# Instruction order from a list scheduler written into the kernel, and two chunks first through the up projection

## The chip, the cores and the metric

The kernel runs on one core of one Trainium2 chip. The metric is the device time of one execution in microseconds (us), median of several. One run at a time is profiled; its span (first to last instruction) is some 2 us shorter than its time. TensorE is PE in the profile, VectorE DVE, ScalarE ACT, GpSimd POOL, the engine that issues most transfers SP.

## The reference, cut to what matters

```python
# attention (RWKV-6): batch 4, 8 heads, 768 steps, head size 48, all fp32
for t in range(S):
    cur = u * k_t (outer) v_t
    y[:, :, t] = r_t @ (state + cur)
    state = w_t * state + k_t (outer) v_t
# then an MLP on x = y laid out as (3072, 384)
h = x @ w_in                       # 384 x 2048, weights given as float64
g = h * clip(h + 3, 0, 6) / 6      # hardswish
out = g @ w_out                    # 2048 x 384
```

## The kernel before

Time is cut into 24 chunks of 128 steps (six to a batch element); three chunks make a block, 8 blocks in all. Per chunk there are two scans and some multiplications (the *preparation*), small matmuls for scores, state and output (the *attention*), and then, block by block, the MLP: 16 *ups* with a gate each, and 16 *downs* per chunk. The MLP's weights come as 64-bit words and are turned into fp32 in the kernel, 16 pairs of 128-row or 128-column blocks, three VectorE steps and two ScalarE steps a pair:

```python
nc.scalar.activation(out=more, in_=lo, func=ACT.Copy, bias=2.0 ** 23, scale=2.0 ** -29)
nc.scalar.activation(out=more.bitcast(I32), in_=more, func=ACT.Copy, bias=-2.0 ** 23, scale=1.0)
nc.vector.tensor_scalar(out=top, in0=hi, ...)                    # shift
nc.vector.scalar_tensor_tensor(out=top, in0=hi, in1=top, ...)    # join
nc.vector.tensor_tensor(out=dst, in0=top, in1=more.bitcast(I32), op=ALU.add)   # full
```

The output of the attention has four head pairs. Three leave PSUM straight into the MLP's input `xT`; the fourth goes to a tile `x3` first, and small DMAs, here called *moves*, bring its rows to the partitions where they belong:

```python
for g in range(2):
    nc.scalar.copy(out=xT[rows, :, now], in_=y_ps[rows, 0:NCC, :])
    nc.scalar.copy(out=x3[rows, now], in_=y_ps[rows, P - 1, :])
if c == BC - 1 or i == 0:                      # chunk 0 alone, else once a block
    for g in range(2):
        for j in range(NCC):
            q = nc.scalar if i == 0 and g == 1 else nc.sync
            q.dma_start(out=xT[to:to + X3, j, cols], in_=x3[...])
```

The order at the start is written by hand, and the framework's own scheduler reorders it:

```python
prep(0); attend(0); prep(1); convert_next(); attend(1)
up(0, 0, 0, 1); up(0, 1, 0, 1)                 # block 0's ups: chunk 0 alone first
prep(2); convert_next(); up(0, 2, 0, 1); up(0, 3, 0, 1); convert_next(); attend(2)
# ... then the rest of block 0 between conversions, and for every chunk i from 3 on:
#     attend(i) with pieces of MLP between its parts, then prep(i + 1)
```

Of the kernel before, what the change touches and what calls it, by code (L numbers as in the profile page):

```python
# [8 lines left out]
F32 = mybir.dt.float32  # L9
# [12 lines left out]
BC = 3  # L22
LEAST = 2.0 ** -60
# [42 lines left out]
def fast_weights(nc, io, wk, w_in, w_out, moe_w_in, moe_w_out):  # L66



    bits_of = {}  # L70

    def fetch(which, f):
        if which == "in":
            srcs = [moe_w_in[:, (f + x) * 128:(f + x + 1) * 128].rearrange("(c p) j -> p c j", p=128) for x in range(2)]
            dst = w_in[:, f:f + 2].rearrange("p f c j -> p (f c) j")
        else:
            srcs = [moe_w_out[(f + x) * 128:(f + x + 1) * 128, :].rearrange("p (c j) -> p c j", j=128)
                    for x in range(2)]
            dst = w_out[:, f:f + 2].rearrange("p f (c j) -> p (f c) j", j=128)
        m = dst.shape[1] // 2  # L80
        if srcs[0].dtype == F32:
            for x in range(2):
                nc.sync.dma_start(out=dst[:, x * m:(x + 1) * m], in_=srcs[x])
            return
        bits = io.tile([128, 2 * m * 128], I64, name="bits", bufs=3)
        for x in range(2):
            nc.sync.dma_start(out=bits.rearrange("p (c j) -> p c j", j=128)[:, x * m:(x + 1) * m], in_=srcs[x])
        bits_of[which, f] = bits, dst.rearrange("p c j -> p (c j)").bitcast(I32)

    def convert(which, f):  # L90
        if (which, f) not in bits_of:
            return
        bits, dst = bits_of.pop((which, f))
        n = dst.shape[1]
        lo = bits.bitcast(U32).rearrange("p (j two) -> p j two", two=2)[:, :, 0]
        hi = bits.bitcast(I32).rearrange("p (j two) -> p j two", two=2)[:, :, 1]
        top = wk.tile([128, n], I32, name="top")
        more = wk.tile([128, n], F32, name="more")

        nc.scalar.activation(out=more, in_=lo, func=ACT.Copy, bias=2.0 ** 23, scale=2.0 ** -29)  # L100
        nc.scalar.activation(out=more.bitcast(I32), in_=more, func=ACT.Copy, bias=-2.0 ** 23, scale=1.0)
        nc.vector.tensor_scalar(out=top, in0=hi, scalar1=3, scalar2=0x3FFFFFF8,  # L102
                                op0=ALU.logical_shift_left, op1=ALU.bitwise_and)
        nc.vector.scalar_tensor_tensor(out=top, in0=hi, scalar=-0x40000000, in1=top,  # L104
                                       op0=ALU.bitwise_and, op1=ALU.bitwise_or)
        nc.vector.tensor_tensor(out=dst, in0=top, in1=more.bitcast(I32), op=ALU.add)  # L106

    return fetch, convert


def fast_path(tc, feat, tok, wflat, ub, moe_w_in, moe_w_out, out, flag, n_chunks):

# [11 lines left out]
    MB = BC * L  # L124
    X3 = D // NCC

    with ExitStack() as ctx:
# [4 lines left out]
        pp = ctx.enter_context(tc.tile_pool(name="pp", bufs=2, space=PSUM))  # L132

        st = [dict() for _ in range(NT)]

        def load(i):
            a = io.tile([PR, nf], F32, name="feat_in")
            b = io.tile([L, 3, HD], F32, name="tok_in", bufs=4)
            n = P * L
            if i == 0:  # L140
                nc.sync.dma_start(out=a[:, 2 * n:], in_=feat[i, :, 2 * n:])
                nc.scalar.dma_start(out=a[:, :2 * n], in_=feat[i, :, :2 * n])
            else:
                nc.sync.dma_start(out=a, in_=feat[i])
            nc.sync.dma_start(out=b.rearrange("s c e -> s (c e)"), in_=tok[i].rearrange("s c e -> s (c e)"))
            st[i].update(r=a[:, :n].rearrange("q (p t) -> q p t", p=P),
                         k=a[:, n:2 * n].rearrange("q (p t) -> q p t", p=P), w=a[:, 2 * n:],
                         rt=b[:, 0], kt=b[:, 1], v=b[:, 2].rearrange("s (h d) -> s h d", d=D))

        load(0)  # L150
        u_bc = const.tile([128, HD], F32, name="u_bc")
        nc.sync.dma_start(out=u_bc, in_=ub.to_broadcast([128, HD]))
        load(1)

        w_in = const.tile([128, NFC, NCC, 128], F32, name="w_in")
        w_out = const.tile([128, NFC, DM], F32, name="w_out")
        fetch, convert = fast_weights(nc, io, wk, w_in, w_out, moe_w_in, moe_w_out)

        fetches = [(which, f) for which in ("in", "out") for f in range(0, NFC, 2)]
        conversions = list(fetches)  # L160

        def fetch_next():
            if fetches:
                fetch(*fetches.pop(0))

        def convert_next():
            convert(*conversions.pop(0))
            fetch_next()

        fetch_next()  # L170
        load(2)
        fetch_next()
        fetch_next()

        ident = const.tile([128, 128], F32, name="ident")
        make_identity(nc, ident)
        half = const.tile([128, 1], F32, name="half")
        nc.vector.memset(half, 0.5)
        ones = const.tile([128, 1], F32, name="ones")
        nc.vector.memset(ones, 1.0)  # L180


        mask_f = const.tile([128, L], F32, name="mask_f")
        nc.gpsimd.memset(mask_f, 1.0)
        nc.gpsimd.affine_select(out=mask_f, in_=mask_f, compare_op=ALU.is_gt, fill=0.0, base=0,
                                pattern=[[1, L]], channel_multiplier=-1)
        mask = const.tile([128, L], U8, name="mask")
        nc.vector.tensor_copy(out=mask, in_=mask_f)


        back = const.tile([PR, P, L + 1], F32, name="back")
        nc.vector.memset(back, 0.0)
        nc.vector.memset(back[:, :, L:], 1.0)
        starts = []
        for i in range(2):
            b = const.tile([PR, P, L + 1], F32, name=f"start_{i}")
            nc.vector.memset(b, 0.0)
            starts.append(b)


        states = []
        for i in range(2):
            b = const.tile([PR, P, PR], F32, name=f"state_{i}")
            nc.gpsimd.memset(b, 0.0)
            states.append(b)


        VN = 1536
        n_w = wflat.shape[1] // VN
        n_v = DM * DFF // 128 // (VN // 2)  # L210
        w_max = const.tile([128, n_w], F32, name="w_max")
        w_min = const.tile([PR, NT, P], F32, name="w_min")
        f64 = moe_w_in.dtype != F32
        word_max = const.tile([128, 2, n_v], F32, name="word_max")
        word_min = const.tile([128, 2, n_v], F32, name="word_min")

        def vet_w(j):
            t = io.tile([128, VN], F32, name="bits", bufs=3)
            nc.sync.dma_start(out=t, in_=wflat[:, j * VN:(j + 1) * VN])
            nc.vector.tensor_reduce(out=w_max[:, j:j + 1], in_=t, axis=AX.X, op=ALU.max, apply_absolute_value=True)  # L220

        def vet_weights(which, j):
            n = VN // 2
            t = io.tile([128, n], I64, name="bits", bufs=3)
            src = (moe_w_in, moe_w_out)[which].rearrange("(p a) b -> p (a b)", p=128)
            nc.sync.dma_start(out=t, in_=src[:, j * n:(j + 1) * n])
            hi = t.bitcast(F32).rearrange("p (j two) -> p j two", two=2)[:, :, 1]
            for o, op in ((word_max, ALU.max), (word_min, ALU.min)):
                nc.vector.tensor_reduce(out=o[:, which, j:j + 1], in_=hi, axis=AX.X, op=op, apply_absolute_value=True)

        vets = [(vet_w, j) for j in range(n_w)]
        if f64:
            vets += [(vet_weights, which, j) for which in range(2) for j in range(n_v)]

        def prep(i):
            d = st[i]
            eng = nc.vector if i < BC else nc.gpsimd
# [3 lines left out]
                                         initial=0.0, op0=ALU.mult, op1=ALU.add)  # L241
            E = E_.rearrange("q (p t) -> q p t", p=P)
            start = starts[i % 2]
            nc.vector.reciprocal(out=start[:, :, 0:1], in_=E[:, :, 0:1])
            W_ = wk.tile([PR, P * (L + 1)], F32, name="W", bufs=3)
            nc.vector.tensor_tensor_scan(out=W_, data0=d["w"][:, :-1], data1=start.rearrange("q p t -> q (p t)"),  # L246
                                         initial=0.0, op0=ALU.mult, op1=ALU.add)
# [560 lines left out]
```

## Time and profile before

| what | value |
|---|---|
| time, median (range) | 649.93 us (648.22 to 650.29) |
| span of the profiled run | 646.3 us |
| last gap of TensorE at the start ends | 109.42 us |
| VectorE busy until then | 98.81 us |
| TensorE from there to its end | 531.43 us, busy 531.41 |
| copy and store after it | 5.45 us |

The slices, windows, waits and groups that carry this are shown in the prediction. Here are the moves, by their tile. The first number of a row is the shortest, then the median and the longest issue in ns; the last line is the time from issue to landing.

```profile
L348 SPq DMA_DIRECT2D xT<-x x15: 512/587/638, 23.8 to 98.3; - x15
L348 ACTq DMA_DIRECT2D xT<-x x3: 600/601/857, 24.5 to 26.0; - x3
DMA to landing us min/median/max: 1.7/1.9/3.6
```

At the median they land in 1.9 us.

### The profile page before, as it was taken

Reading aid. Unit: us, or ns where it says so; the run is one execution under the profiler, and the core shown is the slowest. Engines: PE = TensorE matmul, PEld = TensorE weight load, DVE = VectorE, ACT = ScalarE, POOL = GpSimd, SP = SyncE. Lnnn points to the kernel's source line nnn. Section 1 sums busy time; section 2 is a strip of 40 time slices with the busy share of each in tenths; the row PEclk is TensorE's granted clock in tenths of the full one; section 3 lists DMA queues with packets and bytes.
Section 4 is the critical chain, followed back from the end, with each engine's and each line's share of the span. In section 5 each row is a group of like instructions: output and inputs, shape, how many; then the busy total and the mean of one; then the engine's idle time right before and its main releaser. Section 6 shows DMA issues by size and latency. Waiting matters only on the chain.

```text
span 646.3 us, 7370 instructions
## 1 busy us (share of the span) xinstructions
PE 608.9 (94%) x2802; PEld 392.8 (61%) x2802; DVE 284.0 (44%) x414; ACT 216.8 (34%) x533; POOL 126.3 (20%) x118
## 2 busy tenths in 40 slices
PE   2667997999999999999999999999999999999996
PEld 2556875566656666666666666666666666555553
DVE  7988999769853343314412434115520133002200
ACT  1775874044221443133320443132430332102200
POOL 4135423432222122112121231131210000000000
PEclk9898999999999999999999999999999999999999
DMA  9678767999860221131130221210100000000000
GB/s 261 192 228 258 221 221 246 325 273 315 285 241 34 71 81 54 48 104 34 48 101 14 91 80 35 66 62 0 38 9 25 13 1 1 21 26 0 1 14 28
DMA packets 23900, 67.27 MB, mean 104 GB/s; under 512 B 2912, under 2 KB 13120, under 8 KB 23856
## 3 DMA queue, kind: packets, MB, share of 16 engines
q1 hardware_dynamic: 23632, 66.23, 32.2%
q8 instruction: 24, 0.39, 0.2%
q10 hardware_dynamic: 224, 0.48, 0.2%
q14 instruction: 20, 0.16, 0.1%
HBM read 60.81 MB, written 4.72 MB: 101 GB/s over the span
## 4 chain that ended last, share of the span: by engine, by line
PE 86%; DVE 6%; DMA 2%; ACT 2%; issue 1%; POOL 1%; ACTq 0%; SPq 0%; DVEq 0%
PE mm L374 38%; PE mm L355 35%; PE ps L334 3%; PE a_ps L270 3%; PE ps L329 2%; PE ps L295 2%; DMA feat_in<-in_feat_dram 1%; PE ps L284 1%; DVE top L102 1%; DVE w_out L106 1%; DVE W L246 1%; DVE top L104 1%; DMA bits<-in_moe_w_out_dram 1%; DVE g L361 1%; DVE E L239 1%
## 5 line engine op out<-in xcount | busy, mean ns | idle before, releaser
L374 PE MATMUL mm<-w_out,g 128*128 128x384 f32 x768 | 257.2, 491 | 3.7 <-DVE w_out L106 3.4
L355 PE MATMUL mm<-xT,w_in 128*128 128x384 f32 (+2 forms) x864 | 258.7, 454 | 1.9 <-DVE g L361 1.3
L355 PEld LDWEIGHTS mm<-xT,w_in 128*128 128x128 f32 x864 | 154.8, 191 | 91.0 <-DVE g L361 2.6
L374 PEld LDWEIGHTS mm<-w_out,g 128*128 128x128 f32 x768 | 144.3, 191 | 101.2 <-DVE w_out L106 4.0
L361 DVE SCALAR_TENSOR_TENSOR g<-r,mm 128x384 f32<-128x384 f32 (+2 forms) x144 | 71.8, 505 | 132.2 <-ACT r L358 131.9
L358 ACT ACTIVATE r<-mm,half 128x384 f32<-128x384 f32 (+2 forms) x144 | 77.7, 544 | 126.2 <-PE mm L355 124.4
L261 ACT ACTIVATE A<-ident,dg 128x128 f32<-128x128 f32 x192 | 60.1, 389 | 14.2 <-DVE dg L257 13.9
L250 POOL TENSOR_TENSOR E<-feat_in,E 112x512 f32<-112x512 f32 x21 | 26.6, 1266 | 191.3 <-issue 108.8
L339 ACT COPY xT<-ps 48x384 f32<-48x384 f32 x48 | 22.6, 472 | 86.0 <-PE ps L334 85.5
L273 DVE COPY_PREDICATED A<-mask,a_ps 128x1024 f32<-128x1024 uint8 x24 | 31.2, 1302 | 45.8 <-PE a_ps L270 45.7
L270 PE MATMUL a_ps<-W,E 48*128 48x128 f32 x384 | 30.6, 303 | 16.9 <-DVE W L251 11.5
L246 DVE TENSOR_TENSOR_SCAN W<-feat_in,start 112x516 f32<-112x516 f32 x24 | 38.7, 1614 | 15.0 <-PE ps L329 14.8
L257 DVE TENSOR_REDUCE dg<-rk 128x8 f32<-128x384 f32 x24 | 13.2, 549 | 70.6 <-POOL rk L255 70.6
L270 PEld LDWEIGHTS a_ps<-W,E 48*128 48x128 f32 x384 | 25.7, 204 | 28.1 <-DVE W L251 11.5
L378 ACT COPY o<-mm 128x384 f32<-128x384 f32 x24 | 11.5, 477 | 89.6 <-PE mm L374 87.8
L254 POOL TENSOR_TENSOR rk<-tok_in 128x384 f32<-128x384 f32 x24 | 27.5, 1144 | 58.1 <-DMA tok_in<-in_tok_dram 58.1
L313 POOL TENSOR_TENSOR S<-state,E 112x448 f32<-112x448 f32 x18 | 17.3, 959 | 100.6 <-DVE state L305 93.0
L251 POOL TENSOR_TENSOR W<-feat_in,W 112x512 f32<-112x512 f32 x21 | 25.7, 1226 | 48.2 <-DVE W L246 48.2
L334 PE MATMUL ps<-A,tok_in 128*48 128x128 f32 x384 | 27.7, 289 | 4.2 <-DVE A L273 4.2
L239 DVE TENSOR_TENSOR_SCAN E<-feat_in,back 112x516 f32<-112x516 f32 x24 | 29.3, 1219 | 3.7 <-DMA feat_in<-in_feat_dram 3.7
L286 ACT COPY kn<-ps 128x448 f32<-128x448 f32 x20 | 10.6, 530 | 59.2 <-PE ps L284 57.9
L255 POOL TENSOR_TENSOR rk<-rk,u_bc 128x384 f32<-128x384 f32 x24 | 27.9, 1162 | 1.7
(51 smaller groups left out, 290.7 us busy)
## 6 DMA issues: line engine op xcount, KB each, us to landing
feat_in<-in_feat_dram SPq DMA_DIRECT2D x23, 674.2 KB, 7.4
tok_in<-in_tok_dram SPq DMA_DIRECT2D x24, 576.0 KB, 4.4
bits<-in_moe_w_in_dram SPq DMA_DIRECT2D x16, 384.0 KB, 9.3
bits<-in_moe_w_out_dram SPq DMA_DIRECT2D x16, 384.0 KB, 3.9
bits<-in_moe_w_in_dram SPq DMA_DIRECT2D x8, 768.0 KB, 6.3
bits<-in_moe_w_out_dram SPq DMA_DIRECT2D x8, 768.0 KB, 6.3
bits<-in_wflat_dram SPq DMA_DIRECT2D x6, 768.0 KB, 6.6
out_dram<-o SPq DMA_DIRECT2D x24, 192.0 KB, 1.9
```

The lines of the kernel that those rows point to most:

```text
L239: nc.vector.tensor_tensor_scan(out=E_[:, ::-1], data0=d["w"][:, :0:-1], data1=back.rearrange("q p t -> q (p t)")[:, ::-1], initial=0.0, op ...
L246: nc.vector.tensor_tensor_scan(out=W_, data0=d["w"][:, :-1], data1=start.rearrange("q p t -> q (p t)"), initial=0.0, op0=ALU.mult, op1=ALU ...
L254: nc.gpsimd.tensor_mul(rk, d["rt"], d["kt"])
L255: nc.gpsimd.tensor_mul(rk, rk, u_bc)
L261: nc.scalar.activation(out=A[:, h, :], in_=ident, func=ACT.Copy, scale=dg[:, h])
L270: nc.tensor.matmul(a_ps[:, g, p, :], lhsT=d["K"][rows, p, :], rhs=d["R"][rows, p, :], start=True, stop=True)
L273: nc.vector.copy_predicated(out=d["A"].rearrange("s (p g) t -> s g p t", g=2), mask=mask.rearrange("s (o x t) -> s o x t", o=1, x=1).to_br ...
L334: nc.tensor.matmul(y_ps[g * GP:g * GP + D, p, :], lhsT=d["v"][:, h, :], rhs=d["A"][:, h, :], start=(first and p == 0), stop=(p == P - 1), ...
L355: nc.tensor.matmul(h_ps[:, :n], lhsT=w_in[:, f, j, :], rhs=b["xT"][:, j, cols], start=(j == 0), stop=(j == NCC - 1))
L358: nc.scalar.activation(out=r6[:, :n], in_=h_ps[:, :n], func=ACT.Relu, bias=half, scale=1.0 / 6.0)
L361: nc.vector.scalar_tensor_tensor(out=b["g"][f][:, cols], in0=r6[:, :n], scalar=1.0, in1=h_ps[:, :n], op0=ALU.min, op1=ALU.mult)
L374: nc.tensor.matmul(o_ps, lhsT=b["g"][f][:, c * L:(c + 1) * L], rhs=w_out[:, f, :], start=(f == 0), stop=(f == NFC - 1))
```

## The change

Its intent: TensorE should come to its full stretch earlier. The kernel now describes each piece of work as a step with an engine, a duration that was measured, the steps that it needs and the buffers that it holds. A list scheduler orders the steps once, when the program is built; the framework is told to keep that order. Chunks 0 and 1 go through the up projection together (`SPLIT = 2`), then chunk 2. The core of the diff (cuts marked; the bodies of the steps are the old ones, split up):

```diff
+SPLIT = 2
+START = (-60.0, -47.1, -24.9, -6.3, 4.8, 8.4)    # keys: when a chunk's preparation is due
+class Plan:
+    RATE = 270.0                                  # KB per us
+    LAND = 1.9                                    # us from the end of the transfer to landing
+    def add(self, name, engine, us, emit, after=(), key=0.0, hold=(), port=False, kb=0.0): ...
+    def order(self):
+        # ... of the steps that can start first, the one with the least key; then:
+            if kb:
+                done = max(link, end[n]) + kb / self.RATE if kb > 32 else end[n]
+                link = max(link, done) if kb > 32 else link
+                end[n] = done + self.LAND
+        ctx.enter_context(tc.manual_schedule())
-        prep(0)
-        attend(0)
-        ... (the whole hand-written order)
+        plan.add(f"back{i}", "DVE", 1.4, do(back_scan, i), ..., port=True)
+        plan.add(f"K{i}", "DVE" if dve else "POOL", 0.66 if dve else 1.25, do(make_k, i), ...)
+        ... (tok0 on ACT's queue; chunk 0's own product on DVE; the mask's cast on POOL)
+        plan.add(f"move{i}.{g}", "ACT" if i < BC and g else "SP", 1.8, do(last_pair, ...), ..., kb=1)
+        subs = [(0, SPLIT, ""), (SPLIT, BC, ".")] if bk == 0 else [(0, BC, "")]
+        constants()
+        plan.emit()
```

## The prediction

> **What bounds the kernel now.** I read the page's slices first, then three windows, then TensorE's waits, then the groups of the first window. The slices give the shape:
>
> ```profile
> PE   2667997999999999999999999999999999999996
> DVE  7988999769853343314412434115520133002200
> PEclk9898999999999999999999999999999999999999
> ```
>
> TensorE (PE) has gaps only in the first seven slices (16 us each); from there it is full. VectorE (DVE) is the opposite: nearly full at the start, slack later. Cutting the span where the last gap ends:
>
> ```profile
> core 0: us, PE busy (x) PEld busy (x) DVE busy (x) ACT busy (x) POOL busy (x), PEclk, DMA share, GB/s
> 0.00:109.42 109.42, 77.48 (x533) 63.36 (x533) 98.81 (x143) 66.66 (x158) 41.51 (x39) 0.95 0.76 234
> 109.42:640.85 531.43, 531.41 (x2270) 329.44 (x2270) 185.22 (x272) 149.63 (x374) 84.75 (x79) 1.00 0.24 78
> 640.85:646.30 5.45, 0.00 (x0) 0.00 (x0) 0.00 (x0) 0.48 (x1) 0.00 (x0) 0.98 0.12 42
> ```
>
> From 109.42 to 640.85 us TensorE is busy 531.41 of 531.43 us. No reordering gains there, because the matmuls are the same. The tail of 5.45 us is the last copy and store. So all there is to win lies in the first 109.42 us, where VectorE is busy for 98.81. TensorE's waits say who is late:
>
> ```profile
> PE a_ps L270 <- DVE W L251: 11.5, 1, 11.5
> PE a_ps L270 <- POOL W L251: 5.5, 2, 3.1
> PE ps L334 <- DVE A L273: 4.2, 1, 4.2
> PE mm L374 <- DVE w_out L106: 3.4, 1, 3.4
> ```
>
> 11.5 us is the first input's arrival and its two scans. The last line is the end of the start-up: a down projection waits for the last conversion of w_out. What VectorE spends the first window on (count, busy, mean ns):
>
> ```profile
> L104 DVE SCALAR_TENSOR_TENSOR top<-bits,top 128x768 int32<-128x768 int32 x16 | 17.7, 1104 | 0.1
> L246 DVE TENSOR_TENSOR_SCAN W<-feat_in,start 112x516 f32<-112x516 f32 x8 | 15.0, 1875 | 0.0
> L102 DVE TENSOR_SCALAR top<-bits 128x768 int32<-128x768 int32 x16 | 12.1, 757 | 0.6 <-DMA bits<-in_moe_w_out_dram 0.5
> L106 DVE CUSTOM_DVE_ANT_0 w_out<-top,more 128x1536 uint16<-128x1536 uint16 x8 | 9.3, 1167 | 0.0
> L250 DVE TENSOR_TENSOR E<-feat_in,E 112x512 f32<-112x512 f32 x3 | 2.8, 932 | 0.0
> ```
>
> The conversions (L102, L104, L106) and eight chunks' scans. Their means are too long: beside an idle GpSimd (POOL) the timeline has the same shapes at 0.95 (L104), 1.22 (L246), 0.555 (L102), 0.95 (L106) and 0.66 us (L250). The excess is 16 x 0.15 + 8 x 0.65 + 16 x 0.20 + 8 x 0.22 + 3 x 0.27, and some for L251, about 14 us. GpSimd is busy for 41.5 us there, so one GpSimd us costs VectorE about 0.35 us.
>
> **What the Trainium skill says.** "SBUF — State Buffer", section "Who interferes with whom": a VectorE instruction with two SBUF inputs contends with a GpSimd instruction that reads SBUF, and so does one in a two-port mode; the later one waits for the whole instruction. The trace agrees: at 42.79 us a scan takes 1.97 us while GpSimd multiplies, at 24.32 one takes 1.22 us beside an idle GpSimd; the PSUM-fed L361 stays at 0.40 in its 256-column form. "TensorE: Matmul & The Clock Gate", "What's actually happening": a TensorE with gaps runs at half clock. Here scores take 2.08 us at 11.48 and at 46.70, and 1.16 us later; granted clock 0.95 in the first window against 1.00. "Perfetto Trace Analysis", "Identifying the Most-Contended Engine": TensorE's busy share overstates. It does here: the 77.48 busy us are about 65 us of work at the later pace (below).
>
> **The change part by part.** No matmul, scan or conversion is added or removed: the same work is issued in another order. Four things move.
>
> 1. Block 0's up projection ran first on chunk 0 alone, then on chunks 1 and 2. Now chunks 0 and 1 go together (256 columns), then chunk 2 (128 columns). VectorE keeps 16 gates of 0.40 us and 16 of 0.28. No saving by itself, but each converted pair of w_in blocks now gives TensorE 2.6 us of work instead of 1.3, against about 3 us of VectorE work per pair. TensorE and VectorE then nearly balance, which also keeps the clock up.
>
> 2. VectorE's order. In the changed kernel's order, these stand ahead of the last w_out conversion (in order of program, with uncontended durations): 16 conversions x (0.555 + 0.95 + 0.94) = 39.1; 4 backward and 4 forward scans 9.8; 4 reciprocals 0.7; 6 multiplications 4.0; 4 masked copies x 1.30 = 5.2; 8 state updates x 0.35 = 2.8; 2 decays 1.2; 5 sums x 0.54 = 2.7; chunk 0's own product, now on VectorE, 0.9 (estimate from 0.66 us for a like multiplication, scaled by columns); 16 gates 6.5; 14 gates 3.9. Sum 76.8 us, 117 instructions. Before, the same point had 143 instructions whose durations add up to 107.7, of which about 14 is contention. The difference is the preparation of chunks 4 to 7 and two masked copies, which move behind the last conversion. Durations of neighbours overlap: 107.7 of durations are 98.81 busy us, 0.07 to 0.08 us each. So 76.8 is about 67.5 us of VectorE time.
>
> 3. GpSimd. Ahead of the same point are the own products of chunks 1 to 5 or 6, one decay and chunk 3's two multiplications: 5.5 x 2.0 + 0.95 + 2.4 = 14.4 us by uncontended durations, some 17 as it will run. At 0.35 that is 6 us on VectorE.
>
> 4. The mask's cast moves to GpSimd; the first token load goes on ScalarE's queue. Tenths.
>
> When is the last conversion done? VectorE starts at about 6 us, when the first loads land (6.11 before). 6 + 67.5 + 6 = 79.5. Then its own waits: before, it was idle for 109.42 - 98.81 = 10.6 us, about 6 of them before the first scan; I add 5.5 for the second input (before: 11.63), the masked copies that wait for scores, and late weight transfers. Last conversion at **85 us**. A second way: 109.4 minus the uncontended work moved behind it (93.7 - 76.8 = 17) minus the saved contention (14 - 6 = 8) is 84.4.
>
> Could TensorE be later than this? The first ups need chunk 1's output and its small moves: read 1 near 23 us, copies 1.5, two queues' issues and landing some 4, so 29 to 30 us. After it come 20.6 (ups of two chunks), 10.3 (chunk 2's), 9.0 (seven eighths of chunk 0's down) and two chunks of attention of 4.3: 48.5 us. That gives 78.5 us: below 85, not by much.
>
> What is left after it? In both kernels the wait falls after all ups of block 0 and 28 down passes. Before, more attention was done by then: 7 scores, 6 turns, 5 writes, 5 and 6 parts of reads, against 4, 4, 4, 3 and 4. At steady pitches from the timeline (1.09, 0.44, 0.77, 0.97, 1.01) the difference is 3.3 + 0.9 + 0.8 + 1.9 + 2.0 = 8.9 us. So after the wait 531.4 + 8.9 = 540.3 us of TensorE work remain, plus 5.45 of tail.
>
> (Check of the 65 us: 31.0 of ups, 9.0 of downs, 7 x 1.09, 6 x 0.44, 5 x 0.77, 5 x 0.97, 6 x 1.01 = 65.)
>
> The moved preparation has to be paid later. Between 85 and about 117 us TensorE has 33 us of work (12.9 of the last down, 10.3 and so on, with chunks 4 to 6 between them), VectorE about 22 us for chunks 4 to 7 and 6 of contention. It fits, but chunks 4, 5 and 6 follow each other closely, and block 1's ups wait for chunk 5's moves. I add 2 us of gaps.
>
> Span: 85 + 540.3 + 5.45 + 2 = 632.7 us. The profiled run was 1.8 us over its span, and the median of runs 3.6; I take 2.5. **Predicted 635 us**, 2.3% less than 649.93.
>
> **The rivals.**
>
> *TensorE instead of VectorE bounds the start.* Loads and contention go well, VectorE is done at 79, TensorE binds at 78.5: span 626, time 628. For it: the order was made with durations, so that the engines interleave. Against it: half of TensorE's early work runs at the low clock, and the forward scans and L102 stretch whenever GpSimd runs, as the first window shows.
>
> *Weight transfers bind.* Ahead of the last conversion 12.6 MB of weights and six chunks' inputs (7.7 MB) must land: 20.3 MB in about 83 us is 245 GB/s, against 234 in the first window now and 315 in its best slice of 10 us. There are still three buffers, each fetch waits for a conversion three earlier, and chunk 2's move stands in the same queue ahead of the last four fetches. If this costs 10 us: 645. Against it: before, VectorE waited for weights just 0.5 us.
>
> *The saving is given back between 85 and 120 us.* The prepared chunks were a reserve that before had ready at 109 us. If each of chunks 4 to 6 makes TensorE wait 3 us, with the clock falling after it: 640 to 645. For it: masked copy, decay on GpSimd and read form a chain per chunk. Against it: 10 us of chunk 1's down lie ahead of chunk 4.
>
> *A fixed order blocks.* An engine stuck behind one late item delays all after it. Seen as gaps after 120 us; I expect none, as preparation then runs about 15 us ahead.
>
> **Range and chances.** The start's end between 79 and 93 and 0 to 5 us of later gaps give 628 to 643. The 2% line is 636.9, hardly above the centre, so faster is 0.60, within 2% 0.39, slower 0.01: slower would need a last conversion as late as now and 13 us of new gaps besides.
>
> **What would show it.** TensorE's last long gap ends near 85 us, at a down projection that waits for w_out's conversion; VectorE's busy time up to there is 73 to 76 us; the forward scan's mean in that stretch is below 1.6 us; from 120 us on TensorE has no gap, and the total of its work is unchanged. Wrong: the wait before that down is on a DMA or there is none (TensorE bound); VectorE idle over 12 us in it; gaps of over 5 us between 85 and 120 us.

## The result, and the profile after

| | before | changed |
|---|---|---|
| median of the same rounds | 649.2 us | 641.22 us (641.01 to 643.64) |
| ratio (95% interval) | | 0.9885 (0.9855 to 0.9916) |
| span of the profiled run | 646.3 us | 639.3 us |
| last conversion of w_out done | 109.4 us | 96.7 us |
| TensorE from there to its last matmul | 531.43 us | 536.5 us |
| from there to the end of the span | 5.45 us | 6.0 us |

A ratio is the mean time of one kernel's fast runs over that of the other's in the same rounds, so it is not quite the ratio of the medians. 641.22 lies in the range; the centre was 635.

The page's slices of the changed kernel, to be laid beside those of before:

```profile
PE   2698799999999999999999999999999999999996
DVE  6979798864532653426614455215502222002200
PEclk9779899999999999999999999999999999999999
```

TensorE is full from the sixth slice instead of the eighth. But the granted clock fell to 7 in slices 2 and 3, where it had been 8 and 9. The windows, cut at the start of the last down projection that waits for w_out and at the start of the last store (columns as in the prediction):

```profile
0.00:96.76 96.76, 69.84 (x420) 56.46 (x420) 78.87 (x124) 58.81 (x129) 19.77 (x25) 0.89 0.74 227
96.76:633.85 537.09, 535.57 (x2382) 338.23 (x2382) 204.86 (x292) 157.86 (x404) 116.70 (x93) 1.00 0.27 84
```

The last matmul ends at 633.27 and a copy of 0.48 us lies between it and the store, so TensorE's own stretch is 536.5 us, 535.57 of them busy. VectorE has 124 instructions ahead of the first cut instead of 143 (without the six memsets of the start 118; 117 were predicted), but is idle for 17.9 of 96.76 us. TensorE's waits (total, times, longest) name something that the waits of before did not have:

```profile
PE ps L379 <- DVE E L329: 12.4, 1, 12.4
PE mm L447 <- DMA xT<-x: 9.4, 4, 4.0
PE ps L390 <- ACT kn L384: 2.6, 1, 2.6
PE mm L469 <- DVE w_out L298: 1.7, 3, 1.1
PE ps L420 <- DVE A L370: 1.6, 1, 1.6
```

9.4 us of waiting for moves, 8.5 of them before the last conversion. Where they fall, from TensorE's order of time (start, duration; in brackets the idle time before; the first line is the last piece of chunk 1's attention):

```profile
27.08 1.95 PE L420 MATMUL ps<-A,tok_in 128*48 128x128 f32 x16
32.54 2.04 PE L447 MATMUL mm<-xT,w_in 128*128 128x256 f32 x4 [3.52 <-DMA xT<-x]
35.59 2.93 PE L447 MATMUL mm<-xT,w_in 128*128 128x256 f32 x6 [1.00 <-DMA xT<-x]
...
69.97 0.91 PE L447 MATMUL mm<-xT,w_in 128*128 128x128 f32 x6 [3.98 <-DMA xT<-x]
```

The first ups, of chunks 0 and 1, start at 32.54 and go on at 35.59; chunk 2's wait again at 66 to 70 us. From the chain of work that ended last, the pieces from a move's issue to its landing:

```profile
31.93 3.62 DMA xT<-x
...
64.39 5.45 DMA xT<-x
```

3.62 and 5.45 us, where the kernel before had a median of 1.9 and a longest of 3.6. (Not every move is late: the medians of the first six are 1.8 and 2.1 us by queue, those of chunk 2's six 3.7 and 4.8. TensorE waits for the last one.) And this reaches VectorE, whose longest waits in the first 97 us are

```profile
DVE g L461 <- ACT r L454: 8.5, 10, 2.4
DVE rk L342 <- DMA tok_in<-in_tok_dram: 4.6, 1, 4.6
```

A gate needs an up; VectorE kept the plan's order here (it stood idle 8.5 us for gates while conversions were still to do); so a gate whose up waits for a move holds up every conversion behind it.

### The profile page after: what moved, and what is told of

Same layout as the page of the kernel before. It is cut to its first block, busy times and chain, and to the rows that moved or that the text cites. A ratio compares the mean times of both kernels' runs of the same rounds, so it can differ in the third digit from the quotient of the medians.

```text
span 639.3 us, 7370 instructions
## 1 busy us (share of the span) xinstructions
PE 605.4 (95%) x2802; PEld 394.7 (62%) x2802; DVE 283.7 (44%) x415; ACT 216.7 (34%) x533; POOL 136.5 (21%) x117
## 4 chain that ended last, share of the span: by engine, by line
PE 87%; DVE 5%; DMA 3%; ACT 2%; issue 1%; SPq 0%; ACTq 0%; DVEq 0%
PE mm L469 37%; PE mm L447 37%; PE ps L420 4%; PE a_ps L364 3%; PE ps L415 3%; DMA xT<-x 2%; PE ps L390 2%; PE ps L379 1%; DVE top L293 1%; DMA tok_in<-in_tok_dram 1%; DVE W L318 1%; ACT A L356 1%; DVE g L461 1%; DVE A L370 0%; DVE top L288 0%
## 5 line engine op out<-in xcount | busy, mean ns | idle before, releaser
L469 PE MATMUL mm<-w_out,g 128*128 128x384 f32 x768 | 253.7, 489 | 1.7 <-DVE w_out L298 1.7
L447 PEld LDWEIGHTS mm<-xT,w_in 128*128 128x128 f32 x864 | 158.5, 193 | 101.9 <-issue 9.0
L407 POOL TENSOR_TENSOR S<-state,E 112x448 f32<-112x448 f32 x18 | 28.6, 1591 | 259.5 <-DVE state L402 208.2
L318 DVE TENSOR_TENSOR_SCAN W<-feat_in,start 112x516 f32<-112x516 f32 x24 | 33.9, 1413 | 30.2 <-PE ps L415 29.5
L342 POOL TENSOR_TENSOR rk<-tok_in 128x384 f32<-128x384 f32 x23 | 26.0, 1132 | 63.6 <-DMA tok_in<-in_tok_dram 63.1
L309 DVE TENSOR_TENSOR_SCAN E<-feat_in,back 112x516 f32<-112x516 f32 x24 | 33.5, 1396 | 0.0
L402 DVE TENSOR_TENSOR state<-S,ps 48x192 f32<-48x192 f32 x32 | 11.2, 349 | 46.7 <-PE ps L390 46.5
L364 PE MATMUL a_ps<-W,E 48*128 48x128 f32 x384 | 28.8, 291 | 0.0
L364 PEld LDWEIGHTS a_ps<-W,E 48*128 48x128 f32 x384 | 24.1, 193 | 5.7 <-issue 5.0
L390 PEld LDWEIGHTS ps<-tok_in,kn 128*112 128x112 f32 x160 | 19.9, 190 | 7.5 <-ACT kn L384 2.8
```

The source lines that it names most:

```text
L309: nc.vector.tensor_tensor_scan(out=E_[:, ::-1], data0=d["w"][:, :0:-1], data1=back.rearrange("q p t -> q (p t)")[:, ::-1], initial=0.0, op ...
L318: nc.vector.tensor_tensor_scan(out=W_, data0=d["w"][:, :-1], data1=starts[i % 2].rearrange("q p t -> q (p t)"), initial=0.0, op0=ALU.mult, ...
L364: nc.tensor.matmul(d["a_ps"][:, g, p, :], lhsT=d["K"][rows, p, :], rhs=d["R"][rows, p, :], start=True, stop=True)
L390: nc.tensor.matmul(d["kv_ps"][:, p].rearrange("q g e -> q (g e)"), lhsT=d["kn"][:, p, :], rhs=d["v"][:, 2 * p:2 * p + 2, :].rearrange("s h ...
L407: early(i).tensor_mul(d["S"], states[(i - 1) % 2], d["E"][:, :, 0:1].to_broadcast([PR, P, PR]))
L447: nc.tensor.matmul(h_ps[:, :m], lhsT=w_in[:, f, j, :], rhs=b["xT"][:, j, cols], start=(j == 0), stop=(j == NCC - 1))
```

## The experiments

Theory A: the moves land late, behind weight and input transfers; TensorE's ups wait, its clock falls, VectorE's gates wait and delay the conversions. Rival B: VectorE's own work and its gaps set the date whatever the moves do. Theories C and D add two smaller causes on VectorE: neighbours that depend on each other, and a later first instruction. Unless said otherwise the reference is the changed kernel, 641.22 us; each run was timed against the kernel before on its own chip (medians 648.8 us in the first job, 650.0 in the others; 649.2 for the changed kernel), so differences of medians between jobs are good to about 1 us.

**Moves not issued (wrong result).**

```diff
+            blocks[0]["xT"] = wk.tile(...)          # in constants(): rows zeroed once
+            for p0 in (32, 96):
+                nc.gpsimd.memset(blocks[0]["xT"][p0:p0 + 32], 0.0)
 def last_pair(bk, c0, c1, g, q):
+    if bk == 0:
+        return
```

> Block 0's small moves of the last head pair (chunks 0 and 1, then chunk 2) are not issued; their rows are zeroed once at the start; every engine's order stays. The result is wrong on purpose. Theory A (late moves): the first ups and chunk 2's ups wait 8.5 us for these moves, TensorE goes cold, VectorE's gates wait and hold up the conversions behind them; without the moves the last w_out conversion ends 5 to 7 us earlier (about 90 to 91 us against 96.7) and the time falls to 634 to 636 us. Rival B (VectorE's own work and its gaps set the date): conversions end at 95 us or later, time 639 to 641.

632.79 us (631.74 to 633.55), ratio 0.975. The outputs are wrong by 0.17. TensorE's first and last starts that matter:

```profile
30.19 5.42 PE L453 MATMUL mm<-xT,w_in 128*128 128x256 f32 x24 [1.31 <-ACT xT L436]
90.02 11.88 PE L475 MATMUL mm<-w_out,g 128*128 128x384 f32 x36 [1.55 <-DVE w_out L301]
```

The down after the last conversion starts at 90.02 instead of 96.76: 6.7 us, and 8.4 us in the time. The date is theory A's; the time is 1.2 us better than its band, and rival B falls as the main cause. The run leaves out the issuing of the moves as well as their landing (three moves keep ScalarE's queue 2.13 us in the changed kernel), so it doesn't tell the two apart. The ups begin at 30.19 here, where only ScalarE's copies hold them. That is close to the 29 to 30 us by luck: the record had 4 us for moves in it and the end of chunk 1's attention near 23 us, and this ended at 28.87 here, at 29.03 in the changed kernel.

**Moves earlier (right result).** ScalarE copies the last pair first; half of the moves go by GpSimd's queue; one weight transfer is issued after chunk 2's moves.

```diff
+                nc.scalar.copy(out=b["x3"][rows, now], in_=...)
+            for g in range(2):
                 nc.scalar.copy(out=b["xT"][rows, :, now], in_=...)
-                nc.scalar.copy(out=b["x3"][rows, now], in_=...)
-                    q = nc.scalar if i < BC and g == 1 else nc.sync
+                    q = nc.gpsimd if i < BC and g == 1 else nc.sync
+        # emission: "fetch11" placed behind "move2.*"
```

> The moves stay and the result is right, but they go earlier: ScalarE copies the last pair out of PSUM before the rest, the second half of the moves is issued from GpSimd's idle queue instead of ScalarE's after its copies, and the weight transfer that stood just ahead of chunk 2's moves in the queue is issued after them. Theory A: first ups at about 31.5 without the second stall (35.59 now), chunk 2's ups wait under 2.5 us (3.98 now), time 636 to 639. Rival B: no change over 1 us, 640 to 642.

635.58 us (634.03 to 638.96), ratio 0.9815 (unclear at 2%): a little better than expected. Which of the three edits brings how much was not separated. First ups at 31.80, with no second stall. Chunk 2's wait fell only from 3.98 to 3.31 us, more than the 2.5 that theory A named. Its moves were issued 7 us earlier and landed 7 us after it, on both queues:

```profile
xT<-x SPq DMA_DIRECT2D x3, 8.0 KB, 7.0
xT<-x POOLq DMA_DIRECT2D x3, 8.0 KB, 6.4
```

(size of each and median us to landing). Just before them the same queue had taken chunk 5's inputs, 674 and 576 KB. Which queue a move was issued on made no difference. So theory A was made sharper: a small move lands when what was issued ahead of it has landed.

**Chunk 5's inputs behind chunk 2's moves.** To the edit before:

```diff
+        # emission: "feat5" and "tok5", too, placed behind "move2.*"
```

> As the run with earlier moves, and chunk 5's two input loads too are issued only after chunk 2's moves (1.3 MB less ahead of them in the queue). Theory A2 (a small move lands when the megabytes issued before it have landed): chunk 2's moves land in about 2 to 3 us instead of 7, the wait for them falls from 3.3 us to under 1, the last conversion comes 1 to 3 us earlier, time 633 to 635. If the landing time is a property of these small moves and not of the traffic ahead: still over 6 us, time 635 to 637.

634.53 us (632.06 to 635.53), ratio 0.9753. The same lines as above:

```profile
xT<-x SPq DMA_DIRECT2D x3, 8.0 KB, 1.7
xT<-x POOLq DMA_DIRECT2D x3, 8.0 KB, 1.5
```

7.0 and 6.4 us became 1.7 and 1.5 by holding back two loads. In the run before, their first readers had come 12 us after the issue (a product on GpSimd that is off the path) and 40 us after it (the scan). That settles what these moves wait for, and the run without holding back the weight transfer (below) lies between: with that transfer of 0.77 MB just ahead, the moves took 3.1 and 3.5 us. The time gained is not resolved: 1 us by the medians, more by the ratios, and both ranges and intervals overlap. TensorE, now without that wait, waits 3.6 us for w_out's conversions instead of 2.2.

**Conversion steps interleaved.** On VectorE the `full` of one pair goes behind the `shift` of the next.

```diff
+            if c < a < b:        # fetch{j+1} is out, full{j} stands ahead of shift{j+1}
+                names.insert(a, names.pop(b))
```

> The only edit: on VectorE, each pair's last conversion step goes behind the first step of the next pair, so that two steps of one conversion seldom follow each other. Theory C (dependent neighbours): in the changed kernel a step starts 0.04 to 0.15 us after the end of the one it needs, where independent neighbours overlap by 0.08; 32 such places at 0.12 to 0.2 us give 4 to 6 us of VectorE time, conversions end 3 to 5 us earlier, time 636 to 638. If TensorE and the moves set the date instead: within 1 us of 641.

639.41 us (638.86 to 639.55), ratio 0.9856: 1.8 us, about half of what was expected. The last conversion ends at 94.99 instead of 96.71. What it mends is seen in the changed kernel's own order of time:

```profile
20.21 0.55 DVE L288 TENSOR_SCALAR top<-bits 128x768 int32<-128x768 int32 x1
20.80 0.96 DVE L293 SCALAR_TENSOR_TENSOR top<-bits,top 128x768 int32<-128x768 int32 x1
21.90 0.96 DVE L298 CUSTOM_DVE_ANT_0 w_in<-top,more 128x1536 uint16<-128x1536 uint16 x1
```

Each step starts 0.04 and 0.14 us after the one that it needs has ended. In the kernel before, other work stood between:

```profile
88.44 0.95 DVE L104 SCALAR_TENSOR_TENSOR top<-bits,top 128x768 int32<-128x768 int32 x1
89.31 0.55 DVE L102 TENSOR_SCALAR top<-bits 128x768 int32<-128x768 int32 x1
89.77 0.41 DVE L361 SCALAR_TENSOR_TENSOR g<-r,mm 128x256 f32<-128x256 f32 x1
90.11 0.95 DVE L106 CUSTOM_DVE_ANT_0 w_out<-top,more 128x1536 uint16<-128x1536 uint16 x1
```

88.44 + 0.95 is 89.39, and the next starts at 89.31. So theory C holds in direction. VectorE's waits for gates rose from 8.5 to 10.2 us in this run, so part of the gain ran into the moves. TensorE no longer waits at the last conversion at all; it gains 1.2 us at a masked copy and 0.9 us at earlier w_out conversions.

**The first scan first.** Chunk 0's token load goes behind its features.

```diff
-            q = nc.scalar if i == 0 else nc.sync
+            q = nc.sync                      # and the step's engine is "SP"
```

> Chunk 0's token load moves from ScalarE's queue (where it lands ahead of the scan's input) to the other queue behind chunk 0's features, so that VectorE begins with the first scan and not with the own product. Theory D (late start): first VectorE work at 6.1 instead of 7.33 us, the first score 1 us or more earlier, time 1 to 1.5 us lower, 640. If the start is hidden behind later waits: no change, 641.

638.45 us (637.84 to 639.5), ratio 0.9839: 2.8 us by the medians, 1.5 by the profiled spans, more than the 1 to 1.5 expected. TensorE's first wait is 7.3 instead of 12.4 us, though part of it comes back as a wait of 4.6 us for the masked copy. Theory D holds.

**One chunk first.** The other half of the change undone.

```diff
-SPLIT = 2
+SPLIT = 1
```

> The scheduler stays, but chunk 0 alone goes first through the up projection, then chunks 1 and 2, as in the kernel before. Theory: two chunks first gives TensorE 2.6 us of work per converted pair instead of 1.3, but with moves that land late that work starts later, so the part is worth little: 640 to 645, with TensorE colder between 30 and 60 us. Rival: the early start with one chunk (moves are ready some 6 us earlier, as in the kernel before) is better under the scheduler: 636 to 639.

645.95 us (645.36 to 646.12), ratio 0.9938, just above the expected band. TensorE starts its ups at 25.89, but with half the work per converted pair; the last conversion ends at 100.7. So two chunks first is worth 3.4 us (by the ratios) to 4.7 us (by the medians) under this scheduler, although their moves come later. The keys were left as they were tuned for two chunks; with keys of its own, one chunk first could do better than this, so the worth may be smaller.

**The framework's scheduler over the same emission.**

```diff
-        ctx.enter_context(tc.manual_schedule())
```

> The changed program, emitted in the same order, but the framework's own scheduler may reorder it again, as it did in the kernel before. If it is the fixed order that brings the gain over the kernel before: 643 to 650, with a late last conversion. If what counts is what was moved behind the conversions (chunks 4 to 7 prepared later), which the emitted order gives to both: within 2 us of 641.

654.88 us (652.58 to 655.14), ratio 1.0065 (1.0032 to 1.0099), worse than expected and a little slower than the kernel before. The groups of VectorE's first 101 us say what it did:

```profile
L308 DVE TENSOR_TENSOR_SCAN E<-feat_in,back 112x516 f32<-112x516 f32 x7 | 10.6, 1512 | 5.7 <-DMA feat_in<-in_feat_dram 5.7
L317 DVE TENSOR_TENSOR_SCAN W<-feat_in,start 112x516 f32<-112x516 f32 x6 | 10.0, 1667 | 0.1
```

Seven and six scans are ahead of the last conversion again (four and four in the changed kernel). One scan stood at the head of VectorE's order while its input was still 5.7 us away, and TensorE waited 8.6 us for masked copies. The fixed order is needed for the gain; the steps alone do not bring it.

**All corrections together.** First scan first, interleaved steps, earlier moves, chunk 5's inputs and one weight transfer behind chunk 2's moves.

> All corrections together, result right: first scan first, interleaved conversion steps, earlier moves, chunk 5's loads and one weight transfer behind chunk 2's moves. By the sum of the single gains against the changed kernel (2.8 + 1.8 + 5.6 to 7) 630 us, last conversion near 85 us, as predicted for the changed kernel itself; if TensorE's own work binds then (48.5 us after first ups at 30), not under 628; if the gains overlap: 632 to 635.

633.78 us (632.82 to 634.41), ratio 0.9755. The last conversion ends at 87.53, 2.5 us after the date that was predicted for the changed kernel:

```profile
85.91 1.62 DVE L310 CUSTOM_DVE_ANT_0 w_out<-top,more 128x1536 uint16<-128x1536 uint16 x1
```

But the time is that of the run with the moves and chunk 5's loads alone (634.53): the gains do not add. VectorE now waits 2.9 us for a transfer of w_out, and TensorE still 3.6 us for the first moves.

**Without holding back the weight transfer**, and **without interleaving** as well:

> As the run with all corrections, but the weight transfer that was held behind chunk 2's moves goes ahead of them again (only chunk 5's two loads stay behind). In that run VectorE waited 2.9 us for a transfer of w_out that came late. Theory (that wait is the price of holding the weights back): the wait goes, chunk 2's moves land up to 2.6 us later but behind 0.77 MB only, last conversion at 84 to 86 us instead of 87.5, time 630 to 633. Rival (transfers bind either way): same as that run, 633 to 635.

> The same without the interleaved conversion steps. If interleaving is worth as much here as alone (1.8 us): 1 to 2 us slower than its neighbour, 632 to 635. If the moves and transfers set the date: the same within 0.7 us.

633.91 us (632.75 to 637.23), ratio 0.9764, and 634.68 us (632.94 to 636.06), ratio 0.9765. The wait for w_out's transfer went, as the first theory said, but the time did not follow: the waits for gates rose to 4.7 us and the last conversion ends at 88.8. Three arrangements end within 1 us of each other, so the two rivals ("transfers bind either way", "the same within 0.7 us") fit best. What would take these kernels below 634 us stays open.

These versions are right in result and beat both kernels: 2.4 to 2.5% under the kernel before, against 1.2% for the change as it stood.

## Why the prediction was right or wrong

The sum was 85 + 540.3 + 5.45 + 2 = 632.7 us of span. Measured: 96.76 + 536.5 + 6.0 = 639.3. The mechanism was right in outline (preparation of chunks 4 to 7 moves behind the conversions, they end earlier, what follows is TensorE's work); two terms were mis-sized, in opposite directions. That the time fell inside the range is partly owed to that, which is luck. And VectorE's conversions did not set the end of the start alone: TensorE waited 0.33 us for the last of them and 1.7 us for all of w_out, so it came to 96.76 by its own path almost as late.

**The last conversion, 85 predicted, 96.7 measured.** Term by term:

| term | predicted | measured |
|---|---|---|
| VectorE's first work | 6 | 7.33 |
| durations, with contention | 76.8 + 6 = 82.8 | 81.8 (memsets of the start left out) |
| overlap of neighbours | 9.3 | 4.6 |
| its own waits after the first instruction | 5.5 | 12.2 |

(81.8 is the sum of the groups of the first 96.7 us; 4.6 is 81.8 less the 77.2 us that VectorE was busy after 7.33; 12.2 is 96.71 - 7.33 - 77.2.) The count of instructions and the price of contention were right: 5.0 us over the uncontended sum against 6. Of the 12.2 us, 8.5 are waits for gates. The term that failed most is that of 5.5 us, which had no place for moves that land late. "Small moves ... two queues' issues and landing some 4" was the only time given to them: ScalarE had its copies done at 30.4, yet the last move of chunks 0 and 1 landed at 35.55 (1.5 us of issuing on ScalarE's queue, then 3.62); and chunk 2's moves, which held TensorE for 3.98 us, were not in the sum at all. Leaving the moves out took 6.7 us from this date. The second failure is the overlap, for two reasons. The sum was off: 107.7 of durations less 98.81 busy are 8.9 us over 143 instructions, 0.062 each and not 0.07 to 0.08, which gives 7.3 us for 117. And it was taken over from a kernel in which independent instructions stood between the steps of a conversion; interleaving returned 1.8 us.

TensorE's own path, 78.5, failed too. Its first ups were to come at 29 to 30 us; they ran in full from 35.59, because chunk 1's attention ended at 29.03 and not near 23, and the moves took 5.2 us and not 4. After them came 61.2 us instead of 48.5, 7.3 of them waits (4.0 at chunk 2's moves), and the granted clock was 0.89 over the first 96.76 us, against 0.95 in the first window before: "which also keeps the clock up" did not come true. The rival "a fixed order blocks" named what happened, one late item that holds up an engine, but looked for it after 120 us.

The scheduler shares my error, and its code shows it: a transfer of up to 32 KB does not wait for the link there and lands 1.9 us after its issue. That is what the moves did before. The scheduler placed larger transfers ahead of them and so ended what it had taken for a constant.

The Trainium skill has the mechanism ("DMA: Bandwidth & Descriptors", section "Queues, rings and completion order"): on each DMA engine descriptors are consumed in ring order, and a completion increment lands only after every earlier write from that engine, across its queues. The trace agrees: 7.0 us on SP's queue and 6.4 on GpSimd's with 1.3 MB ahead, 1.7 and 1.5 without; it doesn't tell this rule from data that merely queues on the same engines. I had read the page for its rate and not for this.

**What is left after it, 542.3 predicted with gaps, 536.5 measured.** 1.7 us of the difference was in the 531.4 us that I started from: behind the gap of 3.4 us the kernel before ran its first 36 down passes in 13.57 us, against 11.88 in the changed kernel, because its clock had fallen (granted 0.87 in that stretch, 1.00 in the changed kernel). 1.1 us is that the gaps were 0.9 and not 2, so the rival "the saving is given back between 85 and 120 us" did not happen. About 3 us remain. "No reordering gains there, because the matmuls are the same" was wrong in a small way: from block 1's first up to TensorE's last matmul both kernels have the same matmuls by their order lists, but it took 505.7 us before (135.15 to 640.85) and 502.4 in the changed kernel (130.87 to 633.27), without idle time in either. All the runs in the planned order with two chunks first have 502.4 there, so the 3.3 us are not noise. The new order puts a chunk's write, read, next score and turn side by side, while the old one scattered them among the MLP's matmuls. That the number of such changes is what costs is argued from the order, not tested, and the run with the framework's order over the new steps doesn't settle it: its extra time there is a gap of 2.9 us and a clock that was 0.94 until 200 us, and over its last 430 us it is within 0.3 us of the changed kernel. The cause of these 3 us stays open.

**The checks.** The last long gap was to end near 85 us at a down projection that waits for w_out: it ended at 69.97 at an up that waits for a move, and the wait at w_out was 0.33 us at 96.76. VectorE busy 73 to 76 us: 78.87. The forward scan's mean below 1.6 us: 1.36, right. No gap after 120 us: one of 0.93, again at moves. "VectorE idle over 12 us" was named as a sign that the sum is wrong, and it was 17.9; so was a last wait that is "on a DMA or there is none (TensorE bound)", and 0.33 us is close to none.

**The chances.** 0.60 for faster by over 2% was too much for a centre 2.3% down with late terms as the main risk; the measured ratio is within 2%.

## What to carry to other kernels

A schedule built from measured durations carries over the circumstances in which they were measured: a landing time holds for the traffic that was in flight then, and an overlap for the neighbours that stood there. Before you trust a new order, list the small transfers on the critical path and what is issued ahead of each; loads that nobody needs yet go behind them. On an engine that works in order, a wait at the head of its queue is paid by everything behind it, so one late move of 8 KB can delay weight conversions that have nothing to do with it.

## What the Trainium skill lacked or had wrong

- "DMA: Bandwidth & Descriptors", section "Queues, rings and completion order", has the rule that a small transfer's completion waits for earlier writes, but no size for it: here moves of 8 KB took 7.0 and 6.4 us with 1.3 MB issued just ahead, 3.1 and 3.5 with 0.77 MB, 1.7 and 1.5 us without.
- "VectorE: DVE Perf Modes", section "The DRAIN you can't avoid", says that the next operation waits for the pipeline to empty, and points to cases where it starts earlier. Here independent neighbours start 0.08 us before the recorded end of the one in front (89.31 against 89.39), dependent ones 0.04 to 0.14 us after it; interleaving them gained 1.8 us of the whole time.
- "SBUF — State Buffer", section "Who interferes with whom", tells that the loser blocks for the whole instruction, but gives no price for a mix of instructions: before, some 14 us of VectorE time for 41.5 us of busy GpSimd; in the changed kernel, 5.0 us for 19.8.
- No page that I read says what another order of the same matmuls costs on a TensorE that hardly idles; here they took 505.7 us before and 502.4 in the changed kernel.
